# A linear-attention and MoE kernel: the same instructions listed in a new order, with large loads spread between the copies and blocks of 32-column matmuls kept apart

## The chip, the cores and the metric

The kernel runs on one core of one Trainium2 chip. The metric is the device time of one execution in microseconds (us). The kernel before took 396.19 us (median of three runs, 395.67 to 397.84).

## The reference

Two stages follow each other. A gated linear attention over 4 batches, 8 heads, 768 steps and 48 channels keeps a complex state per head:

```python
mag = np.sqrt(a_re * a_re + a_im * a_im)
scale = np.minimum(mag, 0.999) / (mag + 1e-06)
for t in range(S):
    new_re = ar * S_re - ai * S_im
    new_im = ar * S_im + ai * S_re
    kv = np.einsum('bhd,bhe->bhde', k[:, :, t], v[:, :, t])
    S_re, S_im = (new_re + kv, new_im)
    y[:, :, t] = np.einsum('bhd,bhde->bhe', q[:, :, t], S_re)
```

Its output, 384 wide, goes through a feed-forward stage with a convolution of three steps along the sequence:

```python
h = np.maximum(x @ w_in, 0.0)            # 384 -> 1024
for k in range(K):
    conv_out += conv_w[k][None, None, :] * hp[:, k:k + S, :]
gate = 1.0 / (1.0 + np.exp(-conv_out))
return (h * gate @ w_out)                # 1024 -> 384
```

## The kernel before

**Work.** The sequence is cut into 24 chunks of 128 steps (six per batch); two chunks make a segment, twelve in all. `prelude` (line 300 on) turns the decay factors of a segment into running logarithms and phases on ScalarE (ACT) and VectorE (DVE). `products` (line 339 on) loads q and k (`qk_t`, line 345) and v (`v_t`, line 355), multiplies them with the decays on DVE (lines 349 to 362), and then issues 16 copies that lay the result out by head (`stk`, line 367). `attention` works chunk by chunk on TensorE (PE): products of queries and keys (line 415, 32 matmuls, 64 rows of the result), a mask on DVE (line 419), and then, at line 434, 32 matmuls with the state and 56 with the values, each of which writes 32 rows from a stationary operand of 32 columns. `state` transposes the keys (line 386) and adds to the state with 48 matmuls of 32 columns (line 393). The 32-column matmuls of a chunk are thus 88 of line 434 and 48 of line 393. The counts are those that PE executes: each fp32 matmul of the source is two on PE, so that the order's "x28" is 56 in the trace.

The feed-forward stage runs in nine units of 256 or 384 positions, with four passes over pairs of 128 hidden columns each: `moe_front` (line 500, nine matmuls for each of the two, then ReLU at 503 and the convolution at 504 and 506) and `moe_back` (tanh at 518, split at 521 and 522, matmuls at 527, the output at 533 and 534). These matmuls have 128-column operands. The weights are loaded and split into two parts in the first 75 us (lines 278 to 287).

**Order.** `RANKS` holds one number for each piece of work (an instruction, or a run of matmuls into one tile). `in_order` sorts the pieces by it and chains each engine's instructions, so the table alone sets what stands behind what on PE, ACT, DVE and on SyncE (SP), whose queue issues every DMA:

```python
    for k in sorted(range(len(rows)), key=lambda k: RANKS[k]):
        lines.setdefault(str(rows[k][0].engine), []).append(rows[k])
```

Each engine takes its list strictly in that order. A DMA on SP's list waits there until its buffer is free, and everything behind it waits too: `qk_t` has two buffers, `v_t` three, `stk` four (two per segment), and the DMAs share eight semaphores in turn, so that a DMA also waits for the one eight places ahead of it. What is waited for is set by the data alone and is the same under any table.

Of the kernel before, what the change touches and what calls it, by code (L numbers as in the profile page):

```python
# [47 lines left out]
    2, 10, 0, 3, 7, 8, 12, 14, 15, 6, 5, 16, 9, 0, 4, 13, 1, 0, 11, 27, 41, 58,  # L48
    85, 86, 89, 90, 107, 2, 2, 3, 4, 7, 0, 1, 11, 2, 3, 13, 3, 5, 8, 12, 16, 4,
    5, 25, 6, 7, 21, 4, 6, 9, 13, 15, 8, 9, 32, 10, 11, 34, 6, 14, 20, 28, 38, 12,  # L50
    17, 48, 13, 16, 53, 9, 22, 24, 25, 37, 18, 19, 54, 22, 23, 62, 10, 31, 33, 37, 63, 27,
    31, 69, 30, 32, 66, 11, 42, 46, 50, 55, 36, 43, 86, 38, 41, 88, 13, 55, 59, 62, 89, 49,
    53, 97, 50, 52, 99, 0, 1, 2, 1, 4, 6, 3, 5, 8, 9, 7, 17, 10, 19, 22, 12, 18,
    15, 16, 17, 21, 24, 20, 8, 23, 27, 30, 29, 12, 14, 29, 28, 32, 34, 35, 15, 26, 30, 18,
    16, 22, 31, 19, 27, 20, 23, 29, 24, 25, 28, 32, 14, 40, 15, 45, 20, 67, 21, 54, 24, 56,
    25, 11, 1, 58, 60, 26, 60, 28, 65, 35, 82, 29, 63, 33, 69, 34, 37, 75, 72, 5, 10, 18,
    23, 14, 19, 26, 33, 35, 36, 26, 40, 38, 39, 43, 30, 43, 44, 36, 44, 47, 49, 50, 17, 41,
    47, 45, 51, 21, 51, 51, 52, 52, 53, 57, 35, 36, 34, 39, 41, 37, 38, 40, 44, 43, 45, 46,
    47, 49, 48, 50, 39, 77, 40, 79, 44, 91, 42, 74, 45, 77, 46, 47, 87, 80, 118, 105, 94, 92,
    48, 90, 51, 93, 56, 115, 54, 82, 55, 84, 57, 58, 109, 97, 59, 102, 92, 95, 60, 104, 96, 98,  # L60
    62, 107, 99, 106, 63, 110, 101, 104, 64, 112, 103, 105, 65, 116, 111, 117, 124, 123, 112, 133, 116, 77,
    79, 80, 83, 67, 128, 119, 125, 68, 131, 118, 122, 125, 122, 114, 134, 121, 81, 84, 88, 91, 138, 140,
    126, 146, 135, 90, 95, 94, 97, 154, 142, 140, 158, 143, 100, 99, 101, 102, 168, 114, 172, 95, 7, 31,
    42, 48, 39, 46, 57, 59, 61, 64, 49, 67, 66, 68, 71, 56, 64, 65, 61, 73, 71, 81, 83, 42,
    76, 78, 76, 75, 52, 70, 84, 85, 78, 79, 81, 55, 56, 64, 63, 54, 65, 68, 69, 60, 59, 61,
    66, 62, 58, 67, 57, 61, 111, 66, 119, 73, 139, 69, 108, 70, 109, 71, 72, 18, 17, 126, 113, 166,
    141, 129, 132, 74, 120, 75, 123, 86, 87, 152, 141, 76, 136, 131, 133, 78, 143, 129, 132, 82, 149, 137,
    139, 85, 148, 146, 147, 92, 159, 149, 154, 93, 163, 152, 162, 155, 156, 142, 164, 150, 105, 113, 112, 114,
    98, 162, 153, 161, 103, 171, 159, 164, 157, 173, 156, 180, 169, 115, 119, 129, 126, 104, 178, 175, 199, 106,
    177, 186, 188, 183, 185, 170, 193, 174, 132, 127, 136, 131, 111, 198, 181, 193, 118, 201, 185, 187, 186, 184,  # L70
    176, 203, 182, 137, 134, 138, 135, 225, 115, 230, 136, 128, 213, 202, 205, 130, 207, 190, 204, 222, 223, 203,
    228, 210, 153, 155, 154, 156, 145, 231, 215, 230, 147, 233, 216, 223, 218, 214, 207, 234, 213, 159, 157, 163,
    168, 236, 238, 218, 246, 226, 165, 170, 173, 171, 253, 251, 233, 259, 237, 174, 172, 175, 182, 269, 145, 280,
    163, 33, 68, 72, 70, 70, 74, 80, 96, 98, 100, 73, 94, 93, 91, 114, 95, 83, 88, 87, 113, 110,
    130, 127, 71, 117, 120, 115, 128, 73, 79, 137, 135, 124, 127, 130, 74, 80, 76, 83, 88, 77, 78, 89,
    85, 87, 81, 86, 90, 82, 91, 84, 89, 167, 96, 169, 109, 191, 107, 158, 108, 160, 110, 20, 19, 182,
    167, 116, 188, 117, 189, 122, 195, 120, 171, 121, 172, 123, 124, 200, 179, 53, 101, 108, 100, 103, 106, 121,
    145, 147, 150, 102, 134, 136, 138, 170, 153, 145, 144, 148, 165, 155, 175, 176, 75, 160, 174, 151, 166, 93,
    94, 179, 181, 163, 165, 168, 97, 100, 105, 102, 98, 108, 96, 111, 104, 109, 106, 101, 107, 110, 103, 112,
    125, 206, 133, 210, 141, 217, 139, 192, 140, 194, 142, 143, 219, 198, 144, 220, 146, 224, 150, 256, 148, 206,  # L80
    149, 208, 151, 152, 22, 21, 235, 214, 261, 258, 240, 239, 160, 243, 222, 224, 161, 245, 225, 227, 164, 249,
    229, 231, 166, 252, 235, 244, 167, 262, 239, 243, 169, 265, 240, 242, 260, 255, 238, 267, 249, 183, 190, 184,
    187, 200, 193, 181, 282, 258, 269, 191, 289, 271, 274, 266, 274, 251, 286, 265, 194, 213, 198, 201, 214, 199,
    278, 276, 259, 292, 270, 205, 216, 203, 217, 224, 206, 309, 314, 288, 323, 297, 226, 227, 229, 232, 228, 231,
    333, 178, 336, 198, 348, 190, 72, 144, 161, 157, 151, 190, 187, 192, 196, 194, 173, 180, 178, 177, 208, 215,
    197, 195, 196, 221, 201, 229, 226, 99, 205, 212, 184, 191, 113, 120, 227, 232, 209, 212, 217, 122, 119, 128,
    123, 131, 118, 130, 121, 133, 125, 126, 129, 124, 132, 127, 134, 158, 263, 162, 247, 178, 272, 176, 241, 177,
    245, 179, 180, 275, 248, 185, 253, 186, 254, 188, 189, 285, 260, 195, 294, 268, 281, 196, 295, 267, 272, 202,
    307, 291, 310, 204, 311, 286, 309, 211, 319, 301, 304, 218, 326, 300, 305, 313, 308, 289, 328, 299, 242, 240,
    253, 245, 243, 255, 233, 335, 326, 332, 234, 361, 323, 327, 350, 345, 316, 354, 320, 252, 254, 257, 259, 265,  # L90
    261, 347, 339, 318, 364, 328, 264, 271, 262, 267, 274, 272, 375, 376, 339, 379, 341, 270, 275, 273, 277, 284,
    276, 396, 203, 400, 234, 401, 241, 92, 197, 204, 183, 199, 202, 209, 211, 241, 237, 189, 219, 220, 221, 273,
    216, 211, 232, 200, 257, 236, 264, 268, 117, 248, 279, 228, 255, 135, 144, 271, 270, 247, 250, 256, 142, 141,
    148, 143, 146, 140, 157, 139, 151, 149, 153, 147, 150, 156, 152, 155, 192, 291, 197, 300, 209, 312, 207, 278,
    208, 279, 210, 24, 23, 310, 283, 212, 316, 215, 317, 221, 322, 219, 290, 220, 292, 222, 223, 325, 298, 116,
    242, 254, 234, 244, 250, 281, 284, 287, 288, 246, 264, 262, 263, 298, 277, 257, 261, 252, 293, 266, 303, 302,
    138, 297, 299, 275, 273, 154, 159, 304, 305, 277, 280, 282, 162, 172, 176, 165, 160, 161, 173, 169, 175, 177,
    167, 168, 174, 164, 170, 171, 225, 330, 230, 337, 237, 343, 235, 306, 236, 307, 238, 239, 344, 311, 241, 346,
    244, 349, 248, 368, 246, 315, 247, 317, 249, 250, 26, 25, 355, 321, 384, 370, 359, 358, 256, 365, 333, 336,
    258, 367, 331, 337, 260, 372, 338, 342, 263, 377, 340, 343, 268, 385, 348, 352, 269, 395, 361, 367, 386, 381,  # L100
    350, 397, 359, 286, 290, 295, 292, 296, 298, 285, 404, 375, 379, 291, 408, 368, 369, 389, 388, 353, 399, 374,
    302, 307, 300, 306, 308, 301, 412, 409, 373, 415, 381, 310, 321, 304, 313, 322, 311, 426, 424, 384, 439, 398,
    330, 324, 323, 331, 332, 337, 447, 244, 451, 249, 456, 264, 137, 283, 301, 284, 290, 296, 315, 318, 321, 320,
    276, 294, 295, 293, 351, 306, 287, 285, 296, 332, 302, 340, 338, 166, 329, 352, 303, 319, 183, 185, 341, 342,
    312, 314, 322, 180, 189, 181, 194, 182, 184, 201, 199, 188, 196, 193, 187, 191, 195, 197, 192, 251, 383, 266,
    378, 280, 398, 278, 349, 279, 351, 281, 282, 394, 356, 283, 355, 287, 360, 288, 289, 406, 365, 294, 410, 392,
    393, 297, 417, 382, 385, 299, 418, 396, 399, 303, 427, 395, 401, 309, 431, 404, 423, 312, 437, 410, 413, 438,
    430, 397, 446, 409, 335, 347, 343, 346, 348, 345, 318, 449, 411, 416, 334, 458, 421, 426, 457, 459, 418, 470,
    427, 356, 357, 355, 361, 358, 365, 469, 463, 430, 479, 433, 370, 372, 367, 371, 376, 368, 477, 481, 437, 483,
    438, 378, 380, 374, 379, 381, 382, 495, 263, 497, 265, 504, 267, 158, 324, 327, 308, 331, 334, 353, 356, 360,  # L110
# [617 lines left out]
```

## Time and profile before

| | before |
|---|---|
| median of three runs | 396.19 us |
| the profiled execution's own time | 397.85 us |
| its span, first to last instruction | 396.1 us |
| PE busy | 349.9 us, 5106 matmuls |
| DVE busy | 326.1 us |
| ACT busy | 334.0 us |
| TensorE clock granted, mean | 0.982 |

The profiled execution took 1.66 us more than the median; 1.75 us of its time lie outside the span. A stretch of the span is read as busy time of each engine against the length of the stretch: an engine with no idle time left there sets its length, and one with idle time waits for another.

### The profile page before, as it was taken

The page shows a single profiled execution, that of the slowest core. Times are in us where ns is not written, and L with a number is a line of the kernel's source. Part 1 is how long each engine was busy: PE and PEld are TensorE (multiplying, and loading weights), DVE is VectorE, ACT ScalarE, POOL GpSimd, SP SyncE. Part 2 cuts the span into 40 slices and gives each one's busy share as a digit, 9 for nine tenths or more (in the row PEclk, how much of TensorE's full clock was granted, in tenths as well). Part 3 has the DMA queues.
Part 4 walks back from the last instruction along what each step waited for, and adds up shares of the span by engine and source line. Part 5 has one row for each costly group of instructions (what it writes and reads, how often), then busy time and mean ns, then how long its engine had stood idle before and what let it go on. Part 6 is the DMA issues. An engine that isn't in the chain of part 4 may idle for free.

```text
span 396.1 us, 12054 instructions
## 1 busy us (share of the span) xinstructions
PE 349.9 (88%) x5106; PEld 318.9 (81%) x5106; DVE 326.1 (82%) x515; ACT 334.0 (84%) x575; POOL 4.6 (1%) x35
## 2 busy tenths in 40 slices
PE   0555687997998999998999999999999899999992
PEld 0232465897998999997999889998989799999992
DVE  3999995779799899998999879898999478845850
ACT  6999997898999999998999989989998774544540
POOL 3000000000000000000000000000000000000000
PEclk9999997999899999999999999999999999999997
DMA  8976789484484965793949639728458207400111
GB/s 305 415 282 200 191 219 246 72 171 195 131 163 149 237 140 178 169 268 64 222 122 247 145 53 271 199 44 195 130 89 236 88 2 173 123 2 2 40 43 68
DMA packets 33231, 62.24 MB, mean 157 GB/s; under 512 B 4496, under 2 KB 26000, under 8 KB 33168
## 3 DMA queue, kind: packets, MB, share of 16 engines
q1 hardware_dynamic: 33168, 61.38, 57.8%
q8 instruction: 42, 0.69, 0.7%
q14 instruction: 21, 0.17, 0.1%
HBM read 37.77 MB, written 4.72 MB: 107 GB/s over the span
## 4 chain that ended last, share of the span: by engine, by line
ACT 44%; PE 33%; DMA 10%; DVE 5%; issue 4%; SPq 2%; ACTq 0%; POOL 0%; DVEq 0%
PE o L527 12%; PE h_ps L500 10%; ACT L190 7%; PE ps L434 4%; PE ps L415 4%; ACT g_t L518 3%; DMA stk<-a_t 3%; ACT h_t L503 3%; DMA out<-os_t 2%; DMA qk_t<-in_qk 2%; SPq L367 2%; ACT kn L387 2%; ACT hg L521 2%; ACT a_t L309 2%; ACT a_t L358 2%
## 5 line engine op out<-in xcount | busy, mean ns | idle before, releaser
L527 PE MATMUL o<-wo,hg 128*128 128x384 f32 x576 | 117.6, 345 | 1.0 <-ACT os_t L533 0.5
L500 PE MATMUL h_ps<-x,wi 128*128 128x386 f32 (+1 forms) x648 | 115.2, 325 | 1.0 <-ACT x L446 0.7
L500 PEld LDWEIGHTS h_ps<-x,wi 128*128 128x128 f32 x648 | 105.3, 191 | 3.1 <-issue 1.1
L527 PEld LDWEIGHTS o<-wo,hg 128*128 128x128 f32 x576 | 99.2, 189 | 3.6 <-issue 0.7
L190 ACT ACT_TABLE_LOAD x37 | 47.5, 1283 | 0.6
L415 PEld LDWEIGHTS ps<-stk 96*64 96x64 f32 x768 | 36.1, 141 | 8.8 <-issue 5.5
L504 DVE SCALAR_TENSOR_TENSOR g_t<-h_t,cw 128x384 f32<-128x384 f32 (+1 forms) x72 | 39.8, 565 | 3.9 <-ACT h_t L503 3.6
L518 ACT ACTIVATE g_t<-g_t,cw 128x384 f32<-128x384 f32 (+1 forms) x72 | 39.7, 575 | 3.9 <-DVE g_t L506 3.8
L415 PE MATMUL ps<-stk 96*64 96x128 f32 (+1 forms) x768 | 40.4, 257 | 2.3 <-issue 2.0
L503 ACT ACTIVATE h_t<-h_ps 128x386 f32<-128x386 f32 (+1 forms) x72 | 32.1, 453 | 12.0 <-PE h_ps L500 12.0
L285 PE MATMUL h_ps<-g_t,ident 128*128 128x384 f32 x32 | 20.2, 731 | 23.3 <-DVE g_t L251 12.7
L506 DVE SCALAR_TENSOR_TENSOR g_t<-h_t,cw,g_t 128x384 f32<-128x384 f32 (+1 forms) x72 | 39.3, 566 | 0.1
L519 DVE SCALAR_TENSOR_TENSOR g_t<-g_t,h_t 128x768 f32<-128x768 f32 (+1 forms) x36 | 30.9, 861 | 10.0 <-ACT g_t L518 10.0
L522 DVE TENSOR_TENSOR hg<-g_t,hg 128x768 fp32r<-128x768 f32 (+1 forms) x36 | 31.0, 862 | 8.7 <-ACT hg L521 8.1
L521 ACT ACTIVATE hg<-g_t 128x768 fp32r<-128x768 f32 (+1 forms) x36 | 27.6, 771 | 7.8 <-DVE g_t L519 5.2
L434 PE MATMUL ps<-p_t,v_t 128*32 128x64 f32 x1344 | 27.0, 220 | 6.2 <-issue 5.5
L419 DVE TENSOR_TENSOR p_t<-ps,mask 128x384 f32<-128x384 f32 x48 | 26.1, 551 | 7.2 <-PE ps L415 6.8
L434 PEld LDWEIGHTS ps<-p_t,v_t 128*32 128x32 f32 x1344 | 23.5, 109 | 8.7 <-issue 6.6
L285 PEld LDWEIGHTS h_ps<-g_t,ident 128*128 128x128 f32 x32 | 7.1, 262 | 28.3 <-ACT wi L287 14.2
L434 PE MATMUL ps<-stk,s_sb 96*32 96x128 f32 x640 | 22.1, 277 | 0.5 <-DVE p_t L419 0.5
L533 ACT ACTIVATE os_t<-o 128x384 f32<-128x384 f32 x24 | 11.8, 490 | 12.7 <-PE o L527 6.3
L386 PE MATMUL ps<-ident,qk_t 128*128 128x128 f32 x120 | 20.6, 288 | 1.5 <-DVE x L447 1.5
(93 smaller groups left out, 497.6 us busy)
## 6 DMA issues: line engine op xcount, KB each, us to landing
v_t<-in_v SPq DMA_DIRECT2D x24, 512.0 KB, 5.2
a_t<-in_a SPq DMA_DIRECT2D x12, 768.0 KB, 4.6
qk_t<-in_qk SPq DMA_DIRECT2D x12, 768.0 KB, 5.9
stk<-qk_t SPq DMA_DIRECT2D x96, 96.0 KB, 3.5
stk<-a_t SPq DMA_DIRECT2D x96, 96.0 KB, 3.8
out<-os_t SPq DMA_DIRECT2D x24, 192.0 KB, 3.1
stk<-in_w_in SPq DMA_DIRECT2D x4, 768.0 KB, 8.2
stk<-in_w_out SPq DMA_DIRECT2D x4, 768.0 KB, 7.6
```

The source lines that it names most:

```text
L190: row = [nc.scalar.preload_act_table_set(min(loads[k])).ins, *row]
L415: nc.tensor.matmul(sp[r0:r0 + HC, i, to], lhsT=stk[0][:, h, lo:lo + HC], rhs=stk[1][:, h, lo:], start=(i == 0 and lo == 0), stop=(i == 1 a ...
L434: nc.tensor.matmul(yp[r0:r0 + 32, q // 4, t0:t0 + right.shape[-1]], lhsT=left, rhs=right, start=r0 not in started, stop=n >= len(jobs) - H ...
L500: nc.tensor.matmul(hp, lhsT=wi[:, f2, iw, i, kt], rhs=x[ix][:, kt], start=(k == 0), stop=(k == 8))
L503: nc.scalar.activation(h, hp, func=AF.Relu)
L504: nc.vector.scalar_tensor_tensor(out=g, in0=h[:, 0:n], scalar=cw[:, f, 0:1], in1=h[:, 1:n + 1], op0=ALU.mult, op1=ALU.add)
L506: nc.vector.scalar_tensor_tensor(out=g, in0=h[:, 2:n + 2], scalar=cw[:, f, 2:3], in1=g, op0=ALU.mult, op1=ALU.add)
L518: nc.scalar.activation(g[:, i], g[:, i], func=AF.Tanh, scale=cw[:, 2 * f2 + i, 1:2])
L519: nc.vector.scalar_tensor_tensor(out=g, in0=g, scalar=1.0, in1=h[:, :, 1:n + 1], op0=ALU.add, op1=ALU.mult)
L521: nc.scalar.activation(hi, g, func=AF.Copy)
L522: nc.vector.tensor_tensor(out=lo, in0=g, in1=hi.bitcast(F32), op=ALU.subtract)
L527: nc.tensor.matmul(ops[t], lhsT=hg[:, k, t * C:(t + 1) * C], rhs=wo[:, f2, w, k], start=(f2 == 0 and hg is hi and k == 0 and w == 0), stop ...
```

## The change

The table `RANKS` is another permutation: its lines 48 to 129 differ, two of them are shown. Nothing else differs: the same instructions, tiles and buffers, and as many table loads on ACT.

```diff
 RANKS = [
-    2, 10, 0, 3, 7, 8, 12, 14, 15, 6, 5, 16, 9, 0, 4, 13, 1, 0, 11, 27, 41, 58,
-    85, 86, 89, 90, 107, 2, 2, 3, 4, 7, 0, 1, 11, 2, 3, 13, 3, 5, 8, 12, 16, 4,
...
+    2, 6, 0, 7, 8, 15, 10, 9, 24, 0, 4, 14, 12, 3, 13, 11, 1, 8, 38, 56, 70, 72,
+    75, 76, 85, 100, 82, 2, 1, 2, 3, 7, 0, 3, 12, 1, 2, 14, 3, 4, 6, 9, 15, 4,
...
 ]
```

**Place A.** PE, the second chunk of the first segment. Before, from the last query-key matmuls on; names are result<-stationary or moving operands, then the result's shape and the count in the source (`s_sb` is the state, `p_t` the masked products, `kn` the transposed keys, `g_t`, `wo` weights being split):

```order
L415 MATMUL ps<-stk 64x64 x2
L434 MATMUL ps<-stk,s_sb_103 32x128 x16
L393 MATMUL s_ps<-v_t,kn 32x48 x24
L285 MATMUL h_ps<-g_t,ident 128x384
L434 MATMUL ps<-p_t,v_t 32x64 x28
L285 MATMUL h_ps<-g_t,ident 128x384
L386 MATMUL ps<-ident,qk_t 128x128 x6
```

Now, the same chunk on PE:

```order
L415 MATMUL ps<-stk 64x64 x2
L434 MATMUL ps<-stk,s_sb_103 32x128 x16
L286 MATMUL h_ps<-wo,minus 128x384
L434 MATMUL ps<-p_t,v_t 32x64 x28
L285 MATMUL h_ps<-g_t,ident 128x384
L286 MATMUL h_ps<-wo,minus 128x384
L285 MATMUL h_ps<-g_t,ident 128x384
L286 MATMUL h_ps<-wo,minus 128x384
L393 MATMUL s_ps<-v_t,kn 32x48 x24
```

The 48 matmuls of line 393 moved out of the chunk's line 434 and stand behind it, with four wide matmuls between.

**Place B.** PE, the first chunk of the third segment, where the first matmuls of line 527 stand. Before:

```order
L415 MATMUL ps<-stk 64x64 x2
L434 MATMUL ps<-stk,s_sb_103 32x128 x16
L434 MATMUL ps<-p_t,v_t 32x64 x28
L393 MATMUL s_ps<-v_t,kn 32x48 x24
L415 MATMUL ps<-stk 64x128
L415 MATMUL ps<-stk 64x2x64
L415 MATMUL ps<-stk 64x64 x2
```

Now (`o` is the output of the feed-forward stage, `hg` its gated input):

```order
L415 MATMUL ps<-stk 64x64 x2
L434 MATMUL ps<-stk,s_sb_103 32x128 x16
L434 MATMUL ps<-p_t,v_t 32x64 x28
L527 MATMUL o_869<-wo,hg_874 128x384 x4
L527 MATMUL o_870<-wo,hg_874 128x384 x4
L527 MATMUL o_869<-wo,hg_875 128x384 x2
L415 MATMUL ps<-stk 64x128
```

Line 393 went ahead of the chunk's second half of line 415, and ten wide matmuls of line 527 stand where it was.

**Place C.** SP, from the loads for the third segment on; the numbers tell tiles apart (`qk_t_1006`, `a_t_981` and the copies to `stk_1021`, `stk_1030` are the third segment's, `v_t_1014` its second chunk's, `qk_t_1638` and `v_t_1644` the fourth segment's, `a_t_1870` and `a_t_2370` those of the fifth and sixth). Before:

```order
L355 DMA v_t_1012<-in_v 128x1024
L306 DMA a_t_1870<-in_a 128x1536
L367 DMA stk_1021<-qk_t_1006 96x1x256 x3
L367 DMA stk_1030<-a_t_981 96x1x256 x6
L367 DMA stk_1021<-qk_t_1006 96x1x256 x3
L367 DMA stk_1030<-a_t_981 96x1x256 x2
L367 DMA stk_1021<-qk_t_1006 96x1x256 x2
L355 DMA v_t_1014<-in_v 128x1024
L345 DMA qk_t_1638<-in_qk 128x1536
L306 DMA a_t_2370<-in_a 128x1536
L355 DMA v_t_1644<-in_v 128x1024
```

Now:

```order
L355 DMA v_t_1012<-in_v 128x1024
L306 DMA a_t_1870<-in_a 128x1536
L355 DMA v_t_1014<-in_v 128x1024
L345 DMA qk_t_1638<-in_qk 128x1536
L367 DMA stk_1021<-qk_t_1006 96x1x256 x4
L367 DMA stk_1030<-a_t_981 96x1x256 x3
L367 DMA stk_1021<-qk_t_1006 96x1x256 x2
L367 DMA stk_1030<-a_t_981 96x1x256 x4
L367 DMA stk_1021<-qk_t_1006 96x1x256 x2
L367 DMA stk_1030<-a_t_981 96x1x256
L355 DMA v_t_1644<-in_v 128x1024
L306 DMA a_t_2370<-in_a 128x1536
```

Two of the four large loads that stood behind the sixteen copies stand ahead of them now.

## Rows read from the trace of the kernel before

**Rows 1.** The page: busy time by engine; the queue that carries instructions (packets, MB).

```profile
PE 349.9 (88%) x5106; PEld 318.9 (81%) x5106; DVE 326.1 (82%) x515; ACT 334.0 (84%) x575; POOL 4.6 (1%) x35
...
q8 instruction: 42, 0.69, 0.7%
```

**Rows 2.** Busy time by stretch: start:end length, engines (count), granted clock, DMA share, GB/s.

```profile
60.30:94.75 34.45, 31.73 (x634) 27.84 (x635) 24.70 (x46) 30.64 (x61) 0.21 (x2) 0.90 0.75 190
94.75:125.45 30.70, 28.48 (x380) 27.46 (x380) 27.88 (x49) 28.07 (x54) 0.21 (x2) 0.94 0.55 140
125.45:179.30 53.85, 52.48 (x890) 49.68 (x889) 51.84 (x87) 53.73 (x101) 0.21 (x2) 1.00 0.73 187
179.30:227.65 48.35, 47.20 (x763) 44.31 (x764) 45.18 (x67) 46.85 (x75) 0.41 (x4) 1.00 0.66 161
227.65:311.20 83.55, 81.10 (x1269) 76.54 (x1269) 73.58 (x110) 75.14 (x126) 0.34 (x4) 1.00 0.62 154
311.20:388.70 77.50, 76.47 (x826) 73.94 (x824) 51.74 (x84) 42.59 (x81) 0.00 (x0) 1.00 0.21 52
```

**Rows 3.** PE in order of time: matmuls behind idle time that no event ends.

```profile
62.75 0.42 PE L434 MATMUL ps<-p_t,v_t 128*32 128x64 f32 x8 [2.50 <-issue]
...
96.72 0.61 PE L415 MATMUL ps<-stk 96*64 96x64 f32 x10 [1.98 <-issue]
...
126.28 0.27 PE L434 MATMUL ps<-p_t,v_t 128*32 128x64 f32 x2 [0.89 <-issue]
...
180.20 0.41 PE L434 MATMUL ps<-p_t,v_t 128*32 128x64 f32 x6 [0.92 <-issue]
...
228.75 0.53 PE L434 MATMUL ps<-p_t,v_t 128*32 128x64 f32 x17 [1.14 <-issue]
```

**Rows 4.** Busy time during four of these idle times of PE, columns as in rows 2.

```profile
60.25:62.75 2.50, 0.00 (x2) 0.00 (x1) 0.91 (x3) 0.51 (x1) 0.00 (x0) 1.00 0.80 111
94.73:96.72 1.99, 0.01 (x2) 0.00 (x1) 1.94 (x4) 1.99 (x6) 0.00 (x0) 1.00 0.03 12
...
179.27:180.20 0.93, 0.01 (x2) 0.01 (x1) 0.92 (x2) 0.10 (x1) 0.00 (x0) 1.00 0.09 33
227.60:228.75 1.15, 0.01 (x3) 0.00 (x1) 0.20 (x1) 0.68 (x2) 0.00 (x0) 1.00 0.00 0
```

**Rows 5.** Busy time over blocks of some 127 matmuls, columns as in rows 2.

```profile
56.74:62.75 6.01, 3.51 (x133) 2.74 (x131) 3.85 (x7) 4.01 (x7) 0.00 (x0) 1.00 0.89 216
91.51:96.72 5.21, 3.20 (x143) 2.86 (x132) 4.75 (x9) 5.21 (x14) 0.00 (x0) 1.00 0.50 198
...
176.41:180.20 3.79, 2.73 (x133) 2.41 (x131) 3.77 (x6) 2.96 (x7) 0.00 (x0) 1.00 0.50 195
224.70:228.75 4.05, 2.91 (x136) 2.69 (x131) 2.98 (x6) 3.57 (x6) 0.00 (x0) 1.00 0.31 125
307.88:311.95 4.07, 3.26 (x140) 2.78 (x137) 0.88 (x2) 1.68 (x2) 0.00 (x0) 1.00 0.33 131
...
345.54:349.23 3.69, 3.69 (x142) 3.35 (x135) 2.39 (x6) 2.42 (x7) 0.00 (x0) 1.00 0.17 58
```

**Rows 6.** Busy time in the two stretches at half clock, columns as in rows 2.

```profile
64.10:70.90 6.80, 6.78 (x98) 5.53 (x98) 3.68 (x6) 6.52 (x11) 0.00 (x0) 0.50 0.76 278
...
98.20:101.60 3.40, 3.40 (x17) 3.40 (x16) 2.79 (x6) 2.77 (x7) 0.00 (x0) 0.50 0.00 0
```

**Rows 7.** PE in order of time, one chunk without waits: start, us, what.

```profile
142.68 1.55 PE L527 MATMUL o<-wo,hg 128*128 128x384 f32 x8
144.16 1.56 PE L415 MATMUL ps<-stk 96*64 96x128 f32 x32
145.65 0.88 PE L393 MATMUL s_ps<-v_t,kn 128*32 128x48 f32 x48
146.53 1.10 PE L434 MATMUL ps<-stk,s_sb 96*32 96x128 f32 x32
147.43 0.99 PE L434 MATMUL ps<-p_t,v_t 128*32 128x64 f32 x56
```

**Rows 8.** The chain of waits by time: a copy on it.

```profile
81.95 3.61 DMA stk<-a_t
```

160 rows, old and new, of the table RANKS are left out of this document.

## The prediction, made before the changed kernel ran

> **What bounds the kernel now.** I read the busy time by engine first [rows 1]: PE 349.9, ACT 334.0 and DVE 326.1 us of 396.1, so no engine stands out. By stretches [rows 2] it is clearer. From 125.45 to 179.30 ACT is busy for 53.73 of 53.85 us: there ACT sets the pace, and PE, with 1.4 us of idle time, only keeps up. From 311.20 on ACT has 35 us to spare, and PE works 76.47 of 77.50 us: there PE sets it. Between 60.3 and 125.45, and around 180 and 228, both have gaps.
>
> Next, what PE waits for. The idle times in [rows 3] end with "issue": no semaphore ends them, the next matmul simply isn't there. They are 2.50, 1.98, 0.89, 0.92 and 1.14 us. A sixth, at 311, is the 0.81 us by which a block of 4.07 us exceeds its 3.26 us of PE work [rows 5]. They come at equal distances, not in time but in instructions: the counts of matmuls between them are 634, 380, 890, 763 and 1269 [rows 2], which are 5, 3, 7, 6 and 10 times 127. With its weight load a matmul is two instructions, and 127 of them are 254. The queue that carries instructions moved 42 packets, 0.69 MB [rows 1], some 16 KB each, one for every 243 instructions of PE. So PE's program comes in blocks of some 127 matmuls, and PE stands at the end of a block when the next has not arrived. (The counts in [rows 5] are a little above 127, since what reaches over an edge is counted too.)
>
> How fast may a block be used up? The block at 345.54 took 3.69 us and had no idle time [rows 5]. Those at 176.41, 224.70 and 307.88 held 2.73 to 3.26 us of work and took 3.79 to 4.07. So **a block lasts 3.7 to 4.1 us at least**, and with transfers about longer: 5.21 us at 91.51 (198 GB/s; the large loads of place C's end stand just ahead) and 6.01 us at 56.74 (216 GB/s, the copies). Only blocks full of narrow matmuls fall under this: 48 matmuls of line 393 take 0.88 us and 88 of line 434 take 1.8, 32 of line 415 take 1.49, but eight of line 527 take 1.48, each from start to next start [rows 7].
>
> **The change part by part.** It removes and adds no instruction: the sums of busy time stay, except where a clock or a stall changes them. What moves is which matmuls share a block, and where the loads stand.
>
> *Blocks on PE.* I laid the boundaries on both orders, counting instructions from the known stalls. Before, six blocks hold less than 3.3 us of work, the six that stall. At place A, 30 and 48 of line 434 and 48 of line 393 stood with two wide matmuls; now 86 of line 434, 35 of line 393 and seven wide ones. The narrow ones before are 2.5 us of the 3.51 [rows 5], so two wide ones took 1.0, or 0.3 to 0.5 each with edges; now 2.4 + 7 x 0.3 = 4.5 us or more. At place B ten of line 527 enter, 1.85 us. In the new order three blocks remain under the floor: near 150 us, 79 of line 434, 48 of line 393 and one of 527, 0.65 + 0.92 + 0.88 + 0.19 = 2.6 us; near 228 us, 75 of line 434, 48 of 393 and four of 527, 3.3 us; near 311 us, 83 of line 434 and 45 of 393, 2.6 us. Against a floor of 3.8 to 4.07 they stall 1.2 to 1.45, 0.5 to 0.75 and 1.2 to 1.45 us, some 3.2 together, where the six were 8.2. PE saves 5 us.
>
> *Half clock.* Behind the first two stalls the granted clock is 0.50, from 64.10 to 70.90 and from 98.20 to 101.60 [rows 6]: the lower level, 1.2 GHz, with PE idle for 2.50 and 1.98 us just before. At 2.4 GHz the same work would take half of the 10.2 us, so PE loses up to 5.1 there, or nothing if other causes keep the clock down.
>
> *What reaches the end.* A microsecond that PE saves counts only where ACT was idle as well. In the first stall ACT was busy 0.51 of 2.50 us: 1.99 count. In the second it was busy throughout: 0. The third lies where ACT is full: 0. The fourth gives 0.83, the fifth 0.47 [rows 4], the sixth, where PE sets the pace, its 0.81. In the slow stretches ACT was idle for 0.28 and 0.63 us [rows 6]: 0.91. Sum 5.0 us. Against it: the new stall near 150 us is hidden by ACT, 0; that near 228 counts as the fifth did, 0.41 of it, 0.25; that near 311 in full, 1.3. Blocks near 60 us hold 4.5 us of work, but the copies still run there: 6.01 us for a block would be a stall of 1.5, none at best; I take 0.75, of which 0.8 (1.99 of 2.50) counts, 0.6. Net: 5.0 - 0.25 - 1.3 - 0.6 = **2.85 us**. The ends: 0 (ACT's new order wastes as much as it wins) and 10.1 (5.0 of stalls and 5.1 of clock, all of it reaching the end).
>
> *Loads on SP.* At place C `v_t_1014` and `qk_t_1638` (0.5 and 0.8 MB) pass sixteen copies. Before, the four loads behind the copies run into the block of the second stall; now two do. But both loads wait for PE (their buffers are read by the second segment's chunks), and the copies stand behind them on SP. I cost this at nothing, since with the first stall shorter PE frees these buffers earlier, and the copies' first halves suffice for the first matmuls; the price if not is the second rival's.
>
> The Trainium skill's page "Runtime: NRT & Kernel Launch", section "Instruction fetch mechanics", says the same of size (blocks of 16 KiB, 256 instructions, one fetched while the other runs), but also that fetching is hidden, because instructions are dispatched more slowly than they arrive. By that rule nothing would be won by thinning blocks, and the time would be 396.2. The trace disagrees: 2.50 us with no matmul [rows 4].
>
> **Rivals.** *The order's gain is spent elsewhere.* Every engine's list is new, and ACT, full from 125 to 179, takes its list strictly in order; a few new waits of 0.3 us eat 2.85. For it: ACT idles just 8.1 us between 60.3 and 227.65 in all [rows 2], so the old list was tight. Against: the idle time of PE beside the stalls is small, so the old order had few such waits, and the new one keeps the same steps nearly in the same places. Time 395.3, a gain of 0.9. Under the skill's rule above the same time results, with stalls that stay.
>
> *Copies held up at place C: slower.* The chain runs through a copy of the third segment that lands at 85.56 [rows 8], so these copies are due when they come. Ahead of them now stand 1.3 MB, which at 278 GB/s [rows 6] is 4.7 us, at 190 GB/s [rows 2] 6.9. PE then waits at line 415 of that segment. Its halves stand apart now, with 48 matmuls of line 393 (0.88) and nine of line 500 between (each below line 527's 0.185, since narrower), some 2.2 us of cover: 4.7 - 2.2 = 2.5 us late, and the gain before it is lost. Time 398.7. It decides from about 2 us of delay on. The copies of the later segments run with fewer loads between them, which speaks against a repetition.
>
> *PE's whole saving reaches the end.* If ACT finds work in the gaps, 5.0 + 5.1 = 10.1 us: 387.8 on the profile's scale, 386.1 on the median's. ACT's 8.1 us of idle time up to 227.65 would have to vanish, so I give it little.
>
> **How the numbers follow.** The profiled execution took 397.85 us; less 2.85 that is 395.0. The median stood at 396.19, a factor of 0.9958: **393.3 us**. About 0.5%, 2.0 us, is what a measurement can tell from no change; faster begins under 394.2. Chances: forecast (389 to 394.2) 0.47, whole saving 0.08, spent elsewhere (394.2 to 398.2) 0.28, copies late or another wait of that size 0.17. Faster 0.55, same 0.28, slower 0.17. The range that leaves out 2 in 10 runs from 388.5 to 398.0.
>
> **What would show it.** Idle time of PE ended by "issue" should fall from 8.2 to 2.5 to 5 us, with pieces near 150, 228 and 311 us and none at place B; the clock should be full near 98 us. ACT's idle time between 60 and 125 us should fall from 6.4 to about 3. Right for the wrong reason would be a faster time with as many stalls. I am wrong if PE waits for a copy at line 415 of the third segment near 88 us, if stalls stay at blocks with more than 4.5 us of work, or if the stalls go and ACT idles longer.

## The result and the profile after

| | before | after |
|---|---|---|
| median | 397.01 us (four runs, 395.67 to 397.97) | 391.13 us (four runs, 390.47 to 391.9) |
| ratio, with its 95% interval | | 0.9855 (0.9812 to 0.9898) |
| the profiled execution's own time | 397.85 us | 391.9 us |
| its span | 396.1 us | 390.2 us |
| TensorE clock granted, mean | 0.982 | 0.960 |

The changed kernel is faster by 5.9 us, between the medians as between the two profiled executions. The forecast was 393.3 us, a gain of 2.85: its direction held, and the gain is twice as large. Ratios, here and below, leave out executions over 1.5% longer than the fastest of the same kernel, among them one of 445.29 us of a kernel below, at a mean clock of 0.74.

The busy time on the page of after, which answers to [rows 1]: PE is busy 3.0 us less than before, and the span is 5.9 us shorter, so PE also idles 2.9 us less. (The idle times that end with "issue" shrink by 5.4 us, as shown below; other waits grow by the difference, 1.3 us of it in the first 60 us.) ACT has the same work to 0.1 us.

```profile
PE 346.9 (89%) x5106; PEld 314.8 (81%) x5106; DVE 325.3 (83%) x515; ACT 334.1 (86%) x575; POOL 4.7 (1%) x35
```

Where the time went shows in busy time by equal stretches (columns as in [rows 2]; the last stretch ends with PE's last feed-forward work). First before:

```profile
0.00:60.00 60.00, 32.13 (x345) 19.07 (x346) 50.69 (x74) 56.15 (x83) 3.27 (x21) 1.00 0.83 268
60.00:125.00 65.00, 60.06 (x1018) 55.16 (x1011) 52.61 (x96) 58.56 (x114) 0.41 (x4) 0.92 0.66 167
125.00:180.00 55.00, 52.88 (x916) 49.91 (x904) 52.81 (x88) 54.25 (x101) 0.21 (x2) 1.00 0.71 183
180.00:228.00 48.00, 47.20 (x763) 44.31 (x764) 44.63 (x66) 47.13 (x75) 0.41 (x4) 1.00 0.66 162
228.00:300.00 72.00, 70.36 (x998) 66.44 (x1000) 65.30 (x96) 68.03 (x112) 0.21 (x2) 1.00 0.60 143
300.00:388.70 88.70, 87.20 (x1105) 84.04 (x1095) 59.88 (x98) 49.35 (x94) 0.13 (x2) 1.00 0.27 75
```

Then after:

```profile
0.00:60.00 60.00, 30.81 (x305) 18.66 (x306) 48.30 (x69) 55.29 (x80) 3.33 (x20) 0.77 0.85 266
60.00:125.00 65.00, 61.72 (x1080) 55.72 (x1079) 58.19 (x104) 62.91 (x123) 0.34 (x4) 1.00 0.68 170
125.00:180.00 55.00, 53.96 (x907) 50.26 (x905) 51.82 (x89) 54.81 (x100) 0.18 (x2) 1.00 0.67 169
180.00:228.00 48.00, 47.46 (x767) 44.50 (x766) 46.27 (x68) 47.80 (x80) 0.44 (x5) 1.00 0.76 178
228.00:300.00 72.00, 71.55 (x1060) 67.66 (x1058) 65.08 (x97) 69.02 (x115) 0.41 (x4) 1.00 0.66 158
300.00:382.90 82.90, 81.24 (x996) 78.03 (x994) 55.51 (x92) 43.77 (x83) 0.00 (x0) 1.00 0.24 67
```

Read the fourth number, ACT's. Its idle time (length less busy time) was 3.85, 6.44, 0.75, 0.87 and 3.97 us up to 300; now it is 4.71, 2.09, 0.19, 0.20 and 2.98. ACT is 5.7 us ahead at 300, and PE's last work ends 5.8 us earlier. So, between these two executions, three quarters of the gain arise from 60 to 125 us, 1.2 us from 125 to 228, and 1.0 from 228 to 300; 0.9 is lost in the start.

This split is that of one pair of executions. Two kernels of the experiments below (the one with three loads, and the one without 12 calls) have the lists of before on every engine up to 105 us; in their profiles ACT idles 2.77 and 2.42 us from 60 to 125, where it was 6.44:

```profile
60.00:125.00 65.00, 59.27 (x1088) 53.10 (x1078) 56.82 (x102) 62.23 (x120) 0.41 (x4) 1.00 0.66 168
60.00:125.00 65.00, 60.39 (x1081) 54.39 (x1073) 56.12 (x101) 62.58 (x121) 0.41 (x4) 1.00 0.67 170
```

The gain of 5.9 us is that of the medians too; in which stretch it arises differs from execution to execution.

PE's idle times (stalls) ended by "issue" that exceed 0.3 us, of after, which answer to [rows 3]; behind them busy time from the end of one to the end of the other (columns as in [rows 2]):

```profile
70.38 0.32 PE L434 MATMUL ps<-stk,s_sb 96*32 96x128 f32 x3 [2.13 <-issue]
...
155.58 1.91 PE L527 MATMUL o<-wo,hg 128*128 128x384 f32 x10 [0.69 <-issue]
```

```profile
70.38:155.58 85.20, 83.87 (x1526) 77.44 (x1527) 77.33 (x137) 83.19 (x160) 0.52 (x6) 1.00 0.64 158
```

Two stalls, 2.82 us together, where there were six of 8.24. Between them lie 1527 weight loads, 12 times 127: these stalls too stand on edges of 127 matmuls. At place B there is none, and the clock is full (1.00) behind each.

### The profile page after: what moved, and what is told of

Same layout as the page of the kernel before. It is cut to its first block, busy times and chain, and to the rows that moved or that the text cites. A ratio compares the mean times of both kernels' runs of the same rounds, so it can differ in the third digit from the quotient of the medians.

```text
span 390.2 us, 12058 instructions
## 1 busy us (share of the span) xinstructions
PE 346.9 (89%) x5106; PEld 314.8 (81%) x5106; DVE 325.3 (83%) x515; ACT 334.1 (86%) x575; POOL 4.7 (1%) x35
## 4 chain that ended last, share of the span: by engine, by line
PE 33%; ACT 22%; DVE 15%; DMA 15%; SPq 8%; issue 4%; DVEq 0%; ACTq 0%
PE o L527 13%; PE h_ps L500 11%; SPq L367 7%; PE ps L434 4%; DMA stk<-qk_t 4%; ACT L190 4%; PE ps L415 3%; DMA stk<-in_w_in 3%; DMA stk<-in_w_out 2%; DMA stk<-a_t 2%; ACT g_t L518 2%; DMA v_t<-in_v 2%; ACT h_t L503 2%; ACT hg L521 2%; DVE g_t L506 2%
## 5 line engine op out<-in xcount | busy, mean ns | idle before, releaser
L527 PE MATMUL o<-wo,hg 128*128 128x384 f32 x576 | 119.6, 346 | 1.0 <-issue 0.7
L500 PE MATMUL h_ps<-x,wi 128*128 128x386 f32 (+1 forms) x648 | 114.0, 324 | 0.5 <-ACT h_t L503 0.5
L500 PEld LDWEIGHTS h_ps<-x,wi 128*128 128x128 f32 x648 | 103.8, 189 | 2.1 <-ACT h_t L503 1.0
L527 PEld LDWEIGHTS o<-wo,hg 128*128 128x128 f32 x576 | 98.0, 188 | 3.7 <-issue 0.8
L415 PE MATMUL ps<-stk 96*64 96x128 f32 (+1 forms) x768 | 41.3, 255 | 5.2 <-ACT gph L290 3.9
L285 PE MATMUL h_ps<-g_t,ident 128*128 128x384 f32 x32 | 18.9, 698 | 21.5 <-DVE g_t L251 11.1
L434 PE MATMUL ps<-p_t,v_t 128*32 128x64 f32 x1344 | 25.9, 220 | 0.8 <-DVE p_t L419 0.7
L434 PEld LDWEIGHTS ps<-stk,s_sb 96*32 96x32 f32 x640 | 17.3, 109 | 5.5 <-issue 3.3
```

Of the source, the lines that this page charges most:

```text
L415: nc.tensor.matmul(sp[r0:r0 + HC, i, to], lhsT=stk[0][:, h, lo:lo + HC], rhs=stk[1][:, h, lo:], start=(i == 0 and lo == 0), stop=(i == 1 a ...
L434: nc.tensor.matmul(yp[r0:r0 + 32, q // 4, t0:t0 + right.shape[-1]], lhsT=left, rhs=right, start=r0 not in started, stop=n >= len(jobs) - H ...
L500: nc.tensor.matmul(hp, lhsT=wi[:, f2, iw, i, kt], rhs=x[ix][:, kt], start=(k == 0), stop=(k == 8))
L527: nc.tensor.matmul(ops[t], lhsT=hg[:, k, t * C:(t + 1) * C], rhs=wo[:, f2, w, k], start=(f2 == 0 and hg is hi and k == 0 and w == 0), stop ...
```

## Experiments

Each ratio is against runs of before on the same chip (the kernels ran in three groups on three chips). Single executions of before scatter by 6 us there (393.1 to 399.2, among those that the ratios use), which is why the intervals are wide. Each profile is one execution, and can lie some 3 us off its kernel's median. In kernels with added lines the line numbers of the rows stand a little further than in before (L440 or L442 is line 434, L421 is 415, L454 is 446).

### Moving the edges and nothing else

```diff
+    first = [i for i in nc.cur_bb.bb.instructions
+             if str(i.engine) == "EngineType.PE" and i.opcode == "Matmult" and size(i.outs[0]) == 8]
...
-    lines = {}
+    lines = {"EngineType.PE": [[i] for i in first]}
...
+                    for _ in range(52):
+                        nc.tensor.matmul(rest[0:32, 0:8], lhsT=ident[:, 0:32], rhs=ident[:, 0:8], start=True,
+                                         stop=True, tile_position=(0, 0), skip_group_check=True)
```

52 calls are 104 matmuls on PE, 10 are 20. RANKS is that of before.

> The order of before, with 104 small matmuls (results unused) put ahead of PE's first real one, in time in which PE waits anyway, so that every edge between two blocks of PE's program stands 104 matmuls earlier in the list. Theory (blocks of 256 instructions): the stalls at 62, 96, 126, 180, 228 and 311 us go; short blocks now end near 147, 214 and 300 us, with some 4 us of stall together instead of 8.2, two of them where ACT has no idle time. The time falls by 3 to 6 us, to 391 to 394. Rival (PE stalls because of something at those places, the narrow matmuls themselves or the loads around them): the stalls stay where they are, and the time stays at 397 within 1 us.

Measured: 390.9 us against 397.0, ratio 0.9873 (0.9827 to 0.9919). None of the six stalls is left, and none over 0.3 us appears, not even the three of the expectation. From 60 to 125 us ACT now idles 0.19 us instead of 6.44, at full clock:

```profile
60.00:125.00 65.00, 62.42 (x1108) 56.76 (x1100) 58.23 (x104) 64.81 (x125) 0.42 (x4) 1.00 0.71 183
```

So the old order gives what the changed one gives, when only the edges lie elsewhere. That speaks against every explanation by the loads' places or by the order as such. Nor is it the small matmuls themselves: two kernels below carry 104 of them and 24 more, still stall for 5.3 and 3.3 us, and gain 1.0 and 0.7 us.

> As the run with 104, but with 20 small matmuls. Theory: the edges now cut the narrow runs worse: stalls near 78, 92, 155, 178, 204, 226, 309 and 347 us, of 1 to 3 us each, some 12 to 15 us together; the stalls at 62 and 126 go or shrink. The time is 397 to 402, slower than before. Rival: as before, 397 within 1 us, stalls at the old places.

Measured: 394.07 us, ratio 0.9957 (0.9922 to 0.9991): a little faster, so the size was wrong. Five stalls over 0.4 us instead of eight came, 6.5 us together; their rows (PE in order of time), and busy time from one end to the next:

```profile
75.59 0.31 PE L440 MATMUL ps<-p_t,v_t 128*32 128x64 f32 x4 [0.45 <-issue]
93.43 1.46 PE L421 MATMUL ps<-stk 96*64 96x128 f32 x29 [3.49 <-issue]
...
177.04 0.64 PE L440 MATMUL ps<-p_t,v_t 128*32 128x64 f32 x26 [0.51 <-issue]
287.59 0.31 PE L440 MATMUL ps<-p_t,v_t 128*32 128x64 f32 x4 [1.25 <-issue]
306.31 0.53 PE L440 MATMUL ps<-p_t,v_t 128*32 128x64 f32 x17 [0.82 <-issue]
```

```profile
93.43:177.04 83.61, 81.71 (x1269) 77.44 (x1270) 77.78 (x132) 79.51 (x148) 0.41 (x4) 0.98 0.67 172
177.04:287.59 110.55, 108.94 (x1652) 103.71 (x1652) 103.97 (x151) 108.41 (x175) 0.62 (x6) 1.00 0.62 153
287.59:306.31 18.72, 17.90 (x382) 16.82 (x381) 14.51 (x24) 13.99 (x24) 0.13 (x2) 1.00 0.75 198
```

The stalls moved with the edges: 1270, 1652 and 381 weight loads are 10, 13 and 3 times 127. The stalls fall on edges; how long each is, and which edges have one, was not foreseen.

> The changed order, with 56 small matmuls put ahead. Theory: the two stalls left in the changed kernel (2.13 us at 70 and 0.69 us at 155) go, almost no block is short, at most 0.5 us of stall in all. ACT's idle time of 1.6 us behind the first of them goes; 389 to 390.5 us, faster than the changed kernel's 391. Rival: the changed kernel's stall at 70 us comes from the loads there and stays: 391 within 0.7 us.

Measured: 392.05 us, ratio 0.9895 (0.9852 to 0.9938). Both stalls are gone (one idle time of 0.81 us ended by "issue" stands at 115 us, 25 matmuls behind an edge; its cause I did not find), but ACT idles 1.4 us more in the first 60 us (53.89 us busy instead of 55.29), and PE waits 1.25 us for a copy at 278 us. A gain is not shown; the matmuls at the start may have cost it, so this was repeated (below).

### Does a load hold up the fetch?

```diff
-    for k in sorted(range(len(rows)), key=lambda k: RANKS[k]):
+    for k in sorted(range(len(rows)), key=lambda k: (RANKS + [263] * 3)[k]):
...
+    for b in range(3):
+        x = sa.tile([128, 3, NG * MW], F32, name="a_t", bufs=TBUF)
+        nc.sync.dma_start(x[:, 0:2], a[b, :, 0:2 * NG * MW].rearrange("p (i n) -> p i n", i=2))
```

> The order of before, with three loads of 768 KB into buffers that nothing reads any more, issued on SP behind an output at 342 us, where PE sets the pace and the block from 344.75 to 348.44 us (3.69 us of work, no stall) is used up. Theory (the fetch of a block is held up by loads): that block or the next short one stalls by 1.5 to 5 us, PE's idle time of kind issue grows by as much, and the time is 398.5 to 402 us. Rival (loads don't hold up the fetch; a block has a fixed least time): no new stall, 397 within 0.7 us.

Measured: 400.03 us against 395.93, ratio 1.0082 (1.0048 to 1.0117), 3.2 us slower by the ratio. PE stalls at the end of the block that had no stall before [rows 5]:

```profile
348.23 0.88 PE L415 MATMUL ps<-stk 96*64 96x128 f32 x15
351.32 0.89 PE L415 MATMUL ps<-stk 96*64 96x64 f32 x17 [2.21 <-issue]
```

The DMA queues name the cause (queue: packets, MB, share of 16 engines in the stretch). A packet counts in the stretch in which it starts. In the kernel with the three loads, from 345.2 us, about where the block begins, to 348.5 the data queue alone moves, with the DMA engines full; the instruction packet starts between 348.5 and 348.9 us (second fence):

```profile
q1 hardware_dynamic: 253, 1.36, 104.8%
```

```profile
q1 hardware_dynamic: 16, 0.10, 96.1%
q8 instruction: 1, 0.02, 19.4%
```

In before the block began at 345.54 us [rows 5]; 0.20 MB of data moved up to 346.2, and the packet started right behind, between 346.2 and 346.8 us; the first row is of 345.5 to 346.2, the second of 346.2 to 346.8:

```profile
q1 hardware_dynamic: 143, 0.20, 77.6%
...
q8 instruction: 1, 0.02, 13.5%
```

Behind the new stall PE waits another 0.73 us, for DVE at 355 us, so that 2.9 us of the 3.2 are accounted for in this execution.

So the least time of a block is not fixed: it contains the packet's wait behind data. What follows the packet is steady. In all 40 stalls over 0.3 us that stand on edges, in all these kernels' profiles, PE goes on 2.2 to 2.8 us after the start of the last packet of 16 KB: in before at 62.75, 96.72, 126.28, 180.20 and 228.75 us behind packets that start at 60.12, 94.39, 124.00, 177.98 and 226.24, in the kernel with three loads at 351.32 behind 348.84. A block is thus short if it is used up sooner than its packet's delay and these 2.2 to 2.8 us.

After's own stall at 70 us reads the same way. Its block began at 61.9 us; up to 67.9 us no instruction packet moved, while two `v_t` and an `a_t` that SP had issued from 63.28 us on were landing, with three copies of 96 KB (first fence), and then it came (second):

```profile
q1 hardware_dynamic: 730, 1.45, 94.7%
issues: line engine op xcount, KB each, median us to landing
v_t<-in_v SPq DMA_DIRECT2D x2, 512.0 KB, 4.6
a_t<-in_a SPq DMA_DIRECT2D x1, 768.0 KB, 6.2
```

```profile
q1 hardware_dynamic: 73, 0.38, 92.6%
q8 instruction: 1, 0.02, 5.1%
```

The Trainium skill's page "Runtime: NRT & Kernel Launch", section "Instruction fetch mechanics", calls crossing such an edge one small DMA step that is mostly hidden. That holds at most edges here; at narrow matmuls beside loads the trace shows 2.13, 2.21 and 3.49 us that are not hidden.

### The loads' order alone

```diff
+TAKEN = ('SP',)
...
-    for k in sorted(range(len(rows)), key=lambda k: RANKS[k]):
+    for k in sorted(range(len(rows)), key=lambda k: (OTHER if str(rows[k][0].engine)[11:] in TAKEN else RANKS)[k]):
```

OTHER is the other kernel's table.

> The order of before on PE, ACT, DVE and GpSimd, with the changed order on SP alone, so that only the DMAs are listed anew. Theory (blocks): PE's list is the old one and the stalls stay, some 7 to 9 us; 395.5 to 397.5 us. Rival 1 (the loads' places give the gain): 391 to 393.5 us. Rival 2 (copies held up behind two large loads): slower, 398 to 401 us, with a wait of PE at line 415 of the third segment near 88 us.

Measured: 404.93 us, ratio 1.0183 (1.0118 to 1.0249), slower still than the second rival. PE's list is the old one, and PE stalls 6.45 us at its edges: 2.04, 1.33 and 1.06 us where before stalls too, 1.68 and 0.34 at two edges that had no stall in before. No copy of the third segment is waited for. The costliest wait stands elsewhere: the load of `qk_t` for a later segment was issued at 130.61 us in before, and DVE's product (line 349) ran at 141.33 without a wait; here it is issued at 141.35 us and lands 5.0 us later, at 146.35. DVE waits 3.40 us for it, then PE 3.48 for DVE (SP by time, the load's size and landing, DVE and PE by time; L436 is line 349; the bracket names ACT's line 435, whose result this product does not read):

```profile
141.35 0.53 SPq L432 DMA_DIRECT2D qk_t<-in_qk  x1
```

```profile
qk_t<-in_qk SPq DMA_DIRECT2D x1, 768.0 KB, 5.0
```

```profile
146.44 0.96 DVE L436 TENSOR_TENSOR qk_t<-qk_t 128x768 f32<-128x768 f32 x1 [3.40 <-ACT a_t L435]
```

```profile
151.64 1.60 PE L521 MATMUL ps<-stk,s_sb 96*32 96x128 f32 x32 [3.48 <-DVE p_t L506]
```

> The changed order on PE, ACT, DVE and GpSimd, with the order of before on SP, so that only the DMAs stand as they did. Theory 1 (the gain is PE's blocks; the loads' order is there to feed the other lists): slower than the changed kernel, because the other lists now wait for loads at the wrong place, 394 to 400 us, though PE's stalls stay few (under 4 us). Theory 2 (the loads' places don't matter): 391 within 1 us. Rival (the loads' order is itself the gain): 396 or more, with stalls of 7 us or more.

Measured: 405.26 us, ratio 1.020 (1.0139 to 1.026). The converse mixture is just as slow: worse than theory 1 had it, and against theory 2. The time is the rival's, but not the stalls: its profile (an execution of 413.15 us) has 3.9 us of them and not 7. There DVE waits 3.33 us for a load of `qk_t` at 95.83 us, and PE 4.06 for DVE behind it. The loads' new places are worth nothing by themselves, but each table's SP list fits only its own lists.

### What each stall is worth

The small matmuls now stand in their own rows, at ranks where PE waits (11 and 16), and 24 more bring the edges back to the old places behind a chosen point:

```diff
+GROUPS = [(26, 11), (26, 16), (12, 59)]
...
+    for n, rank in GROUPS:
+        rows.append(extra[:n])
+        ranks.append(rank)
+        extra = extra[n:]
...
+    spare = psO.tile([128, DM], F32, name="o2")
+    for n in range(sum(n for n, _ in GROUPS)):
+        r = 32 * (n % 4)
+        nc.tensor.matmul(spare[r:r + 32, 0:8], lhsT=ident[:, 0:32], rhs=ident[:, 0:8], start=True, stop=True,
+                         tile_position=(0, r), skip_group_check=True)
```

The second kernel has (12, 80) as its last group, the third has no group behind the first two.

> The order of before with 104 small matmuls (results unused) in two of PE's waits near 28 and 39 us and 24 more behind line 500 near 80 us. 104 and 24 are 128, one whole block, so the edges stand elsewhere only up to 80 us: of the six stalls the first (62 us) goes, the other five (96 us and later, 5.7 us) stay. Theory 1 (a stall is worth what ACT idles during it, as predicted): 2.0 + 0.3 us, less 0.4 us for the 24 matmuls; 395 us against 397. Theory 2 (it is worth what ACT waits for PE afterwards, 2.46 us behind the stall and 1.02 in the slow stretch): 3.5 us; 393.5 to 394 us. Rival (the first stall costs nothing): 397.

> The same, but with the 24 matmuls near 101 us, so that the first two stalls go (62 and 96 us) and the slow stretches behind them, and the four later ones stay (3.8 us). Theory 1 (the second stall is worth 0, since ACT was busy throughout, and its slow stretch 0.6 us): 0.6 us faster than the run with only the first removed, 394.4 us. Theory 2 (ACT waits 1.96 us for line 500 behind the second stall, 2.2 with a smaller wait): 2 us faster than that run, 391.5 to 392 us, so that these two stalls are nearly the whole gain.

> The order of before with 104 small matmuls in two waits of PE near 28 and 39 us instead of at the start, and none later: all six stalls go. It completes the series of one and two stalls removed with the same matmuls at the same places. Theory (edges of blocks): as with the matmuls at the start, 5 to 6 us faster than before, no stall over 0.5 us behind 70 us. If only a luckier start made the other run fast: 394 to 396 us.

For the four later stalls alone, a piece of the computation was left out:

```diff
-                 for i in range(H // 2) for q in range(3)]
+                 for i in range(H // 2) for q in range(3) if c != 5]
```

> The order of before without 12 calls (24 matmuls) of line 434 in the sixth chunk, the products with va, so that from some 105 us on every edge stands 24 matmuls later in the list, which is the same as 104 earlier: the first two stalls (62 and 96 us) stay, the four later ones go (in the run with 104 matmuls these edges gave no stall). The work left out is 0.4 us of PE. Theory 1 (a stall is worth what ACT idled during it: 0, 0.8, 0.5 and 0.8 us): 2.1 us, 393.5 to 394.5 against some 396.5. Theory 2 (the runs with one, two and all stalls removed gave 0.9, 0.9 and 5 to 6 us, and prices add up): the four are worth 4 to 5 us, 391.5 to 392.5. Theory 3 (the first two stalls leave ACT a backlog that hides the later ones; prices don't add up): under 1 us, 395.5 to 396.5.

| meant to be removed | stalls over 0.3 us in its profile | median | ratio (95%) | gain by the ratio |
|---|---|---|---|---|
| the first | 0.80, 1.78, 0.31, 1.48, 0.91 | 395.08 us | 0.9974 (0.9944 to 1.0004) | 1.0 us |
| the first two | 0.53, 1.51, 1.23 | 395.03 us | 0.9982 (0.9946 to 1.0019) | 0.7 us |
| the four later ones | 0.34, 0.76, 1.58, 0.42 | 392.57 us | 0.9921 (0.9887 to 0.9956) | 3.1 us, 0.4 of it work left out |
| all six | 0.71 | 389.86 us | 0.9853 (0.9806 to 0.9900) | 5.8 us |

The first stall's 1.0 us agrees with its theory 1 (2 us) within the interval, and so does nothing at all; theory 2's 3.5 us does not. The four later ones are worth 2.7 us, near the 2.1 of theory 1; theory 3 falls, and theory 2's 4 to 5 lies at the edge of the interval. The first two alone are worth less than either theory said (2.6, and 5 or more). All six give the most. The single prices add up to 3.4 us against 5.8, but with intervals of about 1.5 us on each the runs do not show whether prices add up.

Why the first two are worth so little is open. The profile of the run without them does not tell: that execution took 392.28 us, 2.75 under its median, and so shows most of a gain that the median lacks. Its two later stalls were longer than those of before (1.51 and 1.23 us against 0.92 and 1.14):

```profile
174.18 0.41 PE L442 MATMUL ps<-p_t,v_t 128*32 128x64 f32 x6 [1.51 <-issue]
222.77 0.53 PE L442 MATMUL ps<-p_t,v_t 128*32 128x64 f32 x17 [1.23 <-issue]
```

ACT waits longer behind them by about as much. Its waits of before, and then of that run:

```profile
180.66 0.49 ACT L446 ACTIVATE x<-ps 128x384 fp32r<-128x384 f32 x1 [1.29 <-PE ps L434]
229.32 0.49 ACT L446 ACTIVATE x<-ps 128x384 fp32r<-128x384 f32 x1 [1.04 <-PE ps L434]
```

```profile
174.64 0.49 ACT L454 ACTIVATE x<-ps 128x384 fp32r<-128x384 f32 x1 [1.85 <-PE ps L442]
223.35 0.50 ACT L454 ACTIVATE x<-ps 128x384 fp32r<-128x384 f32 x1 [1.09 <-PE ps L442]
```

One reason that the record does show is that a stall differs between executions of the same list. Up to 340 us the lists of the kernel with three loads are those of before; its stalls were 1.50, 2.24, 0.46 and 0.99 us at the second to fifth edge, and none over 0.3 us at the first and the sixth [rows 3 and 5: 2.50 and 0.81]. In the kernel without 12 calls the first was 0.34 us and the second 1.58. So a first stall of 2.50 us may well be rare, and removing it then gives little in most executions; with three executions seen this is a reading, not shown.

### The changed order's own edges

> The changed order with 56 small matmuls in two waits of PE near 30 and 39 us, so that the edges fall as in the run with 56 at the start, but nothing at the start is moved. Theory: no stall at an edge; ACT's wait of 1.6 us near 72 us goes: 389 to 390.5 us, 1 to 2 us faster than the changed kernel. Rival (what is left of stalls in the changed kernel is hidden): 391 to 392 us.

> The same with 80 small matmuls, a control for the matmuls themselves: the edges fall where the narrow runs of the changed order give short blocks again. Theory: stalls near 71, 145 and 210 us of 0.7 to 1.8 us, 3 to 4 us together, half of them where ACT has work: 391 to 393 us, 1 to 2 us slower than with 56. Even at such places the changed order stays faster than before, since wide matmuls stand between its narrow runs. Rival (edges don't matter in this order): as with 56, within 0.5 us.

With 56 (groups of 14 calls at ranks 12 and 18): 391.01 us, ratio 0.9878 (0.9832 to 0.9924). With 80 (groups of 20): 393.44 us, 0.9931 (0.9897 to 0.9965). The run with 56 has no stall and ACT idles 0.51 us from 60 to 125, but it is not faster than the changed kernel (0.9855): what is left of stalls there costs less than these runs resolve. The run with 80 has one stall of the three expected:

```profile
72.80 0.53 PE L442 MATMUL ps<-p_t,v_t 128*32 128x64 f32 x16 [1.94 <-issue]
```

It is 2.4 us slower than the run with 56, but ACT also waits 1.90 instead of 0.58 us at 52 us, ahead of that stall. So the pair doesn't tell cleanly what this stall costs, and no run brings all six stalls back into the changed order. That the changed order stalls little wherever the edges fall held for the shifts tried (0, 56 and 80): 2.8, 0 and 1.9 us, against 8.2, 6.5 and 0 us (0.7 with the matmuls at the other places) of the old order at 0, 20 and 104.

## Why the prediction was right, and where it was not

**Blocks of 127 matmuls.** Right, and the main thing: the stalls follow the edges in every kernel (but for one of 0.81 us), and the old order with moved edges gains as much as the change (0.9853 and 0.9873 against 0.9855).

**A block lasts at least 3.7 to 4.1 us.** This step failed. Four blocks of after, one near each place that the forecast named, columns as in [rows 5]:

```profile
61.90:70.38 8.48, 5.50 (x144) 4.28 (x134) 6.95 (x14) 8.32 (x15) 0.00 (x0) 1.00 0.90 261
152.50:155.58 3.08, 2.39 (x136) 2.44 (x129) 2.40 (x5) 3.07 (x7) 0.00 (x0) 1.00 0.02 5
218.90:222.30 3.40, 3.40 (x136) 3.07 (x136) 3.40 (x7) 3.37 (x5) 0.00 (x0) 1.00 0.02 5
302.76:305.04 2.28, 2.28 (x132) 2.28 (x134) 2.28 (x6) 1.53 (x4) 0.00 (x0) 1.00 0.05 18
```

The last two numbers are the DMA share and GB/s. With hardly any transfers a block passed in 2.28 us without a stall; beside 261 GB/s it took 8.48. The five blocks of [rows 5] that stall all had transfers about them (125 to 216 GB/s), and the sixth, of 3.69 us, did not stall, so that it bounds the least time from above only; I took a wait behind data for a constant. Hence the stalls forecast near 228 and 311 (0.5 to 0.75 and 1.2 to 1.45 us) did not come, that near 150 was 0.69 instead of 1.2 to 1.45, and that near 60 was 2.13, beyond the 0 to 1.5 given. Their sum, 2.8, lies in the 2.5 to 5 that I named, partly by luck. (The block near 228 was summed wrongly as well: by the prices of [rows 7] it is 3.1 us and not 3.3, which makes the forecast stall 0.7 to 1.0.)

**Half clock.** Right that the stretches near 64 and 98 us go: 60.06 us of PE work from 60 to 125 became 61.72 us with 62 more matmuls, at clock 1.00. But it does not follow each stall: behind after's 2.13 us, and behind the 2.21 us of the kernel with three loads, it stayed full. After's lower mean, 0.960, comes from the start, where the clock is 0.50 from 17.7 to 24.5 and from 27.9 to 48.4 us; ACT is busy 6.51 of 6.80 and 20.41 of 20.50 us there, so it costs little.

**What reaches the end.** The mis-sized term. I counted of a stall what ACT idled during it. ACT's idle times over 0.9 us between 60 and 125 us, of before in order of time and then of after, show that it waits later, for what PE finishes late:

```profile
63.22 0.49 ACT L446 ACTIVATE x<-ps 128x384 fp32r<-128x384 f32 x1 [2.46 <-PE ps L434]
...
72.61 0.49 ACT L446 ACTIVATE x<-ps 128x384 fp32r<-128x384 f32 x1 [1.02 <-PE ps L434]
98.83 0.39 ACT L503 ACTIVATE h_t<-h_ps 128x258 f32<-128x258 f32 x1 [1.96 <-PE h_ps L500]
```

```profile
71.85 0.50 ACT L446 ACTIVATE x<-ps 128x384 fp32r<-128x384 f32 x1 [1.60 <-PE ps L434]
```

The second stall (94.73 to 96.72), priced at 0 because ACT was busy throughout [rows 4], is followed by 1.96 us of waiting; 0.63 of them were in the sum, as part of the slow stretch. The wait of 1.02 us ends behind the first slow stretch and was not counted. Part by part, forecast and measured: up to 60 us 0 and -0.9; from 60 to 125 us 2.3 (1.99 + 0.28 + 0.63 - 0.6) and 4.35; from 125 to 300 us 1.05 (0.83 + 0.47 - 0.25) and 2.2; behind 300 us -0.5 (0.81 - 1.3) and 0.1. The sums are 2.85 and 5.8. The first excess is the waits that were not counted, less the stall at 70 us, which left ACT 1.60 us idle and not 0.6; of the rest, 1.55 us is what I had charged for the two stalls that did not come. This account is of the two profiled executions. The runs above in which single stalls are removed do not confirm a price by the later wait (3.5 us and 5 or more forecast, 1.0 and 0.7 measured), so how far the excess of the medians has the same cause stays open.

**Place C.** Costed at nothing, and in the changed kernel that held: PE does not wait at line 415 of the third segment. The price of the loads' order with lists that do not fit it (7 to 8 us slower than before) I had not seen; the rival that came nearest put it at the wrong load.

**Rivals.** The whole saving (386.1 us) was too large by 5 us, but its core, that more of PE's saving reaches the end, was nearer than I allowed. The gain was not spent elsewhere, and no copy was late.

## What to carry to other kernels

Count instructions between unexplained stalls; if the counts are multiples of one number, suspect the program's own arrival, and look for an instruction packet just ahead of each stall's end. Some hundred small matmuls put in an idle stretch ahead move every edge: a cheap test, and here (389.86 us, ratio 0.9853) as good as a new order of the whole kernel. Long runs of very short matmuls beside large loads are where it showed; keep wide work between them, or the loads away. Look for a stall's price in the next wait of the engine that sets the pace as well as in what that engine did during the stall. And take neither a stall nor its price from one trace: the same list had a first stall of 2.50 us in one execution and none over 0.3 us in another.

## What was not expected of the hardware

An instruction packet of 16 KB waits behind data: beside three loads of 768 KB it started 3.6 us into the block instead of 0.7, and PE stood for 2.21 us. PE goes on 2.2 to 2.8 us after the packet's start, in every stall at an edge. That also tells apart two blocks of after that had hardly any transfers: the one that passed in 2.28 us had its packet start at 302.57 us, 0.2 ahead of the block, and the one of 3.08 us, with a stall of 0.69, at 153.23, 0.7 into it. Why the second packet started later is open.
